# First pairs of heads in another order: fillers, gated V loads, flags and masks, and the casts of pair 8

## The chip, the cores and the metric

The kernel runs on one core of one Trainium2 chip. The metric is the device time of one execution in microseconds (us). The engines are TensorE (PE, its weight loads PEld), VectorE (DVE), ScalarE (ACT), GpSimd (POOL) and SyncE (SP, which here only issues transfers). Each works through its own instructions in program order.

## The reference, cut to what matters

Sparse attention over 8 batches x 8 heads, 576 positions, 64 wide, is followed by a two-layer feed-forward part:

```python
scores = scale * np.matmul(q, k.transpose(0, 1, 3, 2))
mask = np.abs(pos[:, None] - pos[None, :]) <= 32
mask = mask | is_global[:, None] | is_global[None, :]   # 8 global positions
attn = softmax(np.where(mask, scores, -1e9))
x = (attn @ v).transpose(0, 2, 1, 3).reshape(4608, 512)
r = np.maximum(x @ w_in, 0.0)            # 512 -> 2048
out = (s * (r * r) + b) @ w_out          # 2048 -> 512
```

All inputs and the output are float32 in DRAM; the 8 global positions are data.

## The kernel before, in words

Work goes by **pairs of heads**: 32 pairs p, four to a batch, and two pairs to a group m. For a pair, Q and K are transposed on TensorE (`trans_a` for K, `trans_b` for Q; from pair 8 on K comes transposed by a DMA instead, `turn_k`), the band of scores is computed in two pieces (`qk(p, 0)`, `qk(p, 1)`), ScalarE takes the exponential (`em`), VectorE multiplies the mask in, and `pvq` multiplies by V and sums; `norm_steps` divides and writes `xt`. The columns and rows of the 8 global positions are handled beside the band: they are gathered with an indirect DMA (`gather`), rounded, moved (`globals_of`) and put into V (`put_v`), K and Q (`put_kq`), and the global queries' rows are written into `xt` by GpSimd (`scatter`).

The feed-forward part is a generator, `moe_quanta`: each `next` (`lead()` in the first pairs, `Q()` later) emits one piece for 512 tokens, either a block of the first layer (psh, then a Relu on ScalarE and a square on VectorE) or a quarter of a block of rows of the second (pso). It fills TensorE between the attention steps.

The order of all engines is **written out by hand**. The first five pairs stand as straight code; from pair 5 on `run_pair` has eight slots a pair, and `at(s, ...)` puts extra steps at the end of slot s, ahead of that slot's piece of the feed-forward part. `later` collects evacuations that `flush` emits. `warm(n)` emits n matmuls on zeros of 128x512, called fillers here, whose result nobody reads; they go to the bank that `idle_bank` names.

**Loads.** SyncE loads V for all pairs and K and Q from pair 8 on (`load_v`, `load_nat`, `load_q`), as float32 in rows of 256 bytes for V and K. GpSimd loads K and Q of pairs 1 to 7 with a cast to bf16 (`load_kq`), the weights (`load_w_in`, `load_w_out`, later `wpiece` for the sum of w_out's rows), and the gathers. SyncE's transfers are on queue 1, GpSimd's on queue 0. The float32 tiles are cast afterwards: V with `cast_v` on VectorE, ScalarE or GpSimd, K with `round_k` and Q with `round_q` on ScalarE. A tile `gate` of one element is loaded by SyncE from `xgs[0]` ahead of V of pair 6; since SyncE issues in order, it holds all loads behind it until `xgs[0]` is written.

`band`, `gadd`, `vkey`, `kidx` (GpSimd) and `sel`, `isg`, `notg` (VectorE) are small tables from which `build_masks` makes the two masks.

Of the kernel before, what the change touches and what calls it, by code (L numbers as in the profile page):

```python
# [16 lines left out]
P = 128  # L17
# [61 lines left out]
def kernel(  # L79
# [186 lines left out]
    zero = const.tile([P, 1], FP32)  # L266
    nc.vector.memset(zero[:], 0.0)
# [10 lines left out]
    load_v(nc.sync, 0)  # L278
# [21 lines left out]
    for p in range(1, 6):  # L300
        load_v(nc.sync, p)
# [4 lines left out]
    load_kq(1)  # L306
    nc.vector.tensor_copy(out=row[:, 0:NG], in_=g32[:, :, 0])
# [52 lines left out]
    nc.gpsimd.memset(kidx[0:NG], 100000.0)  # L360
    vkey = const.tile([P, NCH], FP32)
# [11 lines left out]
    load_kq(2)  # L373
# [9 lines left out]
    gadd = const.tile([P, WM], FP32)  # L383
    nc.gpsimd.memset(gadd[:], 0.0)
    nc.gpsimd.memset(gadd[0:NG, WIN : WIN + P], 1.0)
    nc.gpsimd.memset(gadd[:, GAP : GAP + NG], 1.0)
    nc.gpsimd.memset(gadd[0:NG, GAP : GAP + NG], 0.0)
    load_kq(3)

# [7 lines left out]
    halves("q", nc.scalar.copy, 1)  # L397
    masks = []
# [34 lines left out]
    def globals_of(bb):  # L433
# [26 lines left out]
        def move(i):  # L460
            ps = bank("psv")
            ps = ps.rearrange("p (a h d) -> p a h d", a=4, h=2)
            for hp in range(4):
# [4 lines left out]
                lambda: nc.vector.tensor_copy(  # L468
# [67 lines left out]
    def trans_b(p, later=later):  # L536
        ps = trans("q", p)

        def evac():
            n = HB // NJ  # L540
            eng = A if p < 5 else V
# [212 lines left out]
    def lead():  # L754
        next(moe)
# [77 lines left out]
    def idle_bank():  # L833
        return fill[:, 0:DM]
# [31 lines left out]
    def turned(f, p):  # L866
# [4 lines left out]
    fill = ps_o.tile([P, 2 * DM], FP32, tag="o", name="psf")  # L871
    warm(7)
# [4 lines left out]
    )  # L877
    halves("k", nc.vector.tensor_copy, 0)
# [7 lines left out]
    rows_of(0)  # L886
    k_out = turned(trans_a, 0)
    warm(2)
    q_out = turned(trans_b, 0)
    put = select(0)  # L890
    warm(2)
    k_out()
    put()
    q_out()
    sel = const.tile([P, NCH, NG], FP32)
    nc.vector.tensor_tensor(
        out=sel[:], in0=view(kidx[:], [1, NCH], [0, NG]),
        in1=view(gidx_f, [0, NCH], [1, NG]), op=OP.is_equal,
    )
    isg = const.tile([P, NCH], FP32)  # L900
    nc.vector.tensor_reduce(out=isg[:], in_=sel[:], axis=AX.X, op=OP.add)
    notg = const.tile([P, NCH], FP32)
    nc.vector.tensor_tensor(out=notg[:], in0=vkey[:], in1=isg[:], op=OP.is_gt)
# [18 lines left out]
    for p in range(3):  # L922
        qk(p, 0)
        q_out = turned(trans_b, p + 1)
        warm((2, 2, 1)[p])
        if p == 0:
            for g in range(2):
                build_masks(g)
            nc.vector.memset(onesb[:], 1.0)
# [4 lines left out]
        warm((2, 1, 1)[p])  # L934
        k_out()
        put()
        flush()
        if p:
            cast_v(V, p - 1)
    qk(3, 0)  # L940
    turned(trans_b, 4)()
    qk(3, 1)
    mask_b = later.pop()
    flush()
    steps0[0]()
    steps0[2]()
    flush()
    put_v(V, 0)
# [196 lines left out]
```

## Time and profile before

| | |
|---|---|
| median of 3 runs | 351.9 us (350.98 to 353.53) |
| profiled execution | 352.85 us, its span 351.2 us |
| busy share of the span | PE 95%, PEld 48%, DVE 60%, ACT 59%, POOL 18% |
| transfers | 50.25 MB in 124,452 packets, mean 143 GB/s |
| on the chain that ended last | PE 71%, DMA 15%, DVE 5%, SyncE's queue 4%, ACT 2% |

The span is the time from the first to the last instruction that the profile shows. Busy time of matmuls is modelled at their ends. The chain is followed back from the last instruction, at each step to what released it.

### The profile page before, as it was taken

The page shows a single profiled execution, that of the slowest core. Times are in us where ns is not written, and L with a number is a line of the kernel's source. Part 1 is how long each engine was busy: PE and PEld are TensorE (multiplying, and loading weights), DVE is VectorE, ACT ScalarE, POOL GpSimd, SP SyncE. Part 2 cuts the span into 40 slices and gives each one's busy share as a digit, 9 for nine tenths or more (in the row PEclk, how much of TensorE's full clock was granted, in tenths as well). Part 3 has the DMA queues.
Part 4 walks back from the last instruction along what each step waited for, and adds up shares of the span by engine and source line. Part 5 has one row for each costly group of instructions (what it writes and reads, how often), then busy time and mean ns, then how long its engine had stood idle before and what let it go on. Part 6 is the DMA issues. An engine that isn't in the chain of part 4 may idle for free.

```text
span 351.2 us, 8783 instructions
## 1 busy us (share of the span) xinstructions
PE 333.5 (95%) x3433; PEld 170.2 (48%) x3433; DVE 211.0 (60%) x553; ACT 205.9 (59%) x347; POOL 64.0 (18%) x151
## 2 busy tenths in 40 slices
PE   8968999699999998899999999999999999999996
PEld 4545444344454544357644444444456544444444
DVE  5589777466748596647666767675757553513421
ACT  3455687538875787437874887488638604603600
POOL 7733832141003310130006000300020010000000
PEclk9985899999999999989999999999999999999999
DMA  7999999999989999999579998992730011011002
GB/s 156 198 207 198 197 209 190 201 169 225 170 183 143 221 211 165 210 134 173 91 151 252 184 173 183 240 196 58 153 112 2 2 63 61 0 62 60 1 32 89
DMA packets 124452, 50.25 MB, mean 143 GB/s; under 512 B 111378, under 2 KB 117714, under 8 KB 124402
## 3 DMA queue, kind: packets, MB, share of 16 engines
q1 hardware_dynamic: 115992, 38.45, 62.3%
q0 software_dynamic: 8064, 10.80, 16.3%
q8 instruction: 27, 0.44, 0.6%
q10 hardware_dynamic: 354, 0.43, 0.4%
q14 instruction: 15, 0.12, 0.1%
HBM read 42.35 MB, written 9.44 MB: 147 GB/s over the span
## 4 chain that ended last, share of the span: by engine, by line
PE 71%; DMA 15%; DVE 5%; SPq 4%; ACT 2%; issue 1%; POOL 0%; ACTq 0%; DVEq 0%
PE psh L687 31%; PE pso L721 29%; DMA natv<-in_v_dram 7%; DMA wst<-in_moe_w_out_dram 5%; PE po L592 5%; PE pss L568 4%; SPq L203 3%; DMA natq<-in_q_dram 2%; DVE wsum L1013 2%; DMA kt<-natb 1%; PE pst L501 1%; DVE xt L639 1%; ACT em L575 1%; PE psx L592 1%; DVE g L712 1%
## 5 line engine op out<-in xcount | busy, mean ns | idle before, releaser
L687 PE MATMUL psh<-xt,win_t 128*128 128x512 bf16 (+2 forms) x704 | 134.9, 342 | 0.6 <-DVE kt L527 0.6
L721 PE MATMUL pso<-wout_t,g 128*128 128x512 bf16 (+1 forms) x592 | 134.3, 377 | 0.0
L709 ACT ACTIVATE r<-psh 128x512 bf16<-128x512 f32 x144 | 85.3, 599 | 65.2 <-PE psh L687 64.4
L687 PEld LDWEIGHTS <-win_t 128*128 128x128 bf16 x704 | 62.4, 98 | 57.7 <-issue 3.0
L721 PEld LDWEIGHTS <-g 128*128 128x128 bf16 x592 | 55.2, 98 | 61.1 <-issue 1.7
L712 DVE TENSOR_TENSOR g<-r 128x512 bf16<-128x512 bf16 x144 | 60.9, 430 | 38.0 <-ACT r L709 37.1
L575 ACT ACTIVATE em<-pss 128x904 bf16<-128x904 f32 (+1 forms) x61 | 54.7, 897 | 39.9 <-PE pss L568 39.9
L576 DVE TENSOR_TENSOR em<-em,mask 128x904 bf16<-128x904 bf16 x64 | 39.0, 614 | 23.4 <-ACT em L575 23.3
L664 POOL COPY xt<-xg 128x4 bf16 (+1 forms) x72 | 18.0, 250 | 176.3 <-DVE xt L639 172.5
L741 DVE SCALAR_TENSOR_TENSOR osb<-pso,sb,bias_row 128x512 f32<-128x512 f32 (+1 forms) x25 | 18.1, 726 | 27.3 <-PE pso L721 27.2
L568 PE MATMUL pss<-qt,kt 64*128 64x160 bf16 (+1 forms) x366 | 22.9, 234 | 4.3 <-DVE qt L486 2.3
L568 PEld LDWEIGHTS <-kt 64*128 64x128 bf16 x384 | 11.6, 98 | 30.1 <-issue 15.9
L639 DVE TENSOR_TENSOR xt<-po,rep 128x480 bf16<-128x480 f32 (+2 forms) x60 | 24.4, 447 | 0.0
L646 ACT ACTIVATE ln<-po 128x324 f32<-128x324 f32 (+1 forms) x30 | 12.8, 426 | 10.7 <-PE po L592 10.7
L592 PE MATMUL po<-em,vring 128*32 128x160 bf16 (+3 forms) x840 | 18.0, 224 | 1.0 <-DVE vring L478 0.9
L214 ACT CAST natb<-natk 128x640 bf16<-128x640 f32 x24 | 17.4, 725 | 2.2 <-DMA natk<-in_k_dram 2.2
L543 DVE COPY qt<-pst 128x600 bf16<-128x600 bf16 x19 | 8.8, 464 | 11.8 <-PE pst L501 11.8
L592 PE MATMUL po<-em,onesb 128*32 128x192 bf16 (+2 forms) x360 | 11.8, 238 | 4.0 <-DVE xt L639 3.9
L592 PEld LDWEIGHTS <-vring 128*32 128x32 bf16 x896 | 14.6, 102 | 1.5 <-DVE vring L478 1.5
L649 ACT ACTIVATE rep<-ln 128x324 f32<-128x324 f32 (+1 forms) x32 | 14.7, 460 | 0.2
L1013 DVE TENSOR_TENSOR wsum<-wsum,wst 128x512 f32<-128x512 f32 x14 | 9.6, 685 | 7.5 <-DMA wst<-in_moe_w_out_dram 7.4
L238 ACT CAST sixq<-natq 120x640 bf16<-120x640 f32 x19 | 13.8, 729 | 0.0
(117 smaller groups left out, 217.5 us busy)
## 6 DMA issues: line engine op xcount, KB each, us to landing
natv<-in_v_dram SPq DMA_DIRECT2D x59, 150.0 KB
natk<-in_k_dram SPq DMA_DIRECT2D x47, 150.0 KB
out_dram<-osb SPq DMA_DIRECT2D x23, 256.0 KB
natq<-in_q_dram SPq DMA_DIRECT2D x37, 150.0 KB
wst<-in_moe_w_out_dram POOLq DMA_DIRECT2D x8, 512.0 KB, 6.8
out_dram<-osbh SPq DMA_DIRECT2D x9, 256.0 KB
win_t<-in_moe_w_in_dram POOLq DMA_DIRECT2D x4, 512.0 KB, 9.4
wout_t<-in_moe_w_out_dram POOLq DMA_DIRECT2D x4, 512.0 KB, 10.9
```

The costliest lines, as they stand in the source:

```text
L214: nc.scalar.copy(out=natb[:, p % NV].rearrange("p (c h d) -> p c h d", c=NCH, h=2), in_=natk[:, p % NV],)
L568: nc.tensor.matmul(ps[:, hh, at : at + hi - lo], ktile[p][r, P * c : P * c + P], qbufs[p % 3][r, lo:hi], start=at == 0, stop=at + hi - lo ...
L575: nc.scalar.activation(em[:], ps[:, :, 0:n], AF.Exp, scale=SCALE)
L576: later.append(lambda: nc.vector.tensor_mul(em[:], em[:], masks[g]))
L592: nc.tensor.matmul(po[DH * j : DH * j + DH, a : a + n], view(vring[:, p % NVR, c, hh, part - 1 :], [2, DH]) if part else onesb[:], emt[(p, ...
L639: nc.vector.tensor_tensor(out=view(xt[:, 2 * g, x0 + t0 :], [NXT, 2], [w, runs], [1, w]), in0=view(po[:, STEP[blk] + col :], [STEP[blk], 2 ...
L664: nc.gpsimd.tensor_copy(out=xt[:, h, S * (bi % NX) : S * (bi % NX) + S][:, :, ds(greg_p[i], 1)], in_=xgs[bi][:, h, i : i + 1],)
L687: nc.tensor.matmul(psh[:, d0 : d0 + n], win_t[:, a, f * P : f * P + P], xt[:, a, x0 : x0 + n], start=(a == 0 and j == 0), stop=(a == 3), s ...
L709: nc.scalar.activation(r[:], psh, AF.Relu)
L712: later.append(lambda g=g, r=r: nc.vector.tensor_mul(g[:], r[:], r[:]))
L721: nc.tensor.matmul(pso[:, 0:nn], gl[f][:, u * P : u * P + P], wout_t[:, f, n0 : n0 + nn], start=(f == 0), stop=(f == 15),)
L741: nc.vector.scalar_tensor_tensor(out=osb[:, 0:nn], in0=pso[:, 0:nn], scalar=s_bc, in1=bias_row[:, n0 : n0 + nn], op0=OP.mult, op1=OP.add,)
```

## The change

- The unused tile `zero` goes, so `dummy` is set first. The fillers ahead of the first scores become 5 + 2 in place of 7 + 2 + 2; those in the loop over the first pairs become one each in place of 2, 2, 1 and 2, 1, 1. Eight new ones stand further on: one between the two scores of pair 3, three ahead of `put_out(0, 0)`, three behind the transposes of pair 4's K, and one behind `steps0[1]`; those after pair 3 go to a bank of `ps_s`.
- SyncE loads V of pairs 0 to 5 behind a new gate, one element of K of pair 1, in place of V of pair 0 first and the others after the constants.
- On GpSimd the loads of pairs 2 and 3 move ahead of `vkey` and `band`; `gadd` moves to VectorE; the load of pair 6 moves ahead of the first scatter.
- `rows_of(0)` comes after the copy of pair 0's K. `gadd`, `sel`, `isg` and `notg` are made by `key_flags` on VectorE, in pair 0's turn of the loop at its end, with the masks behind it; pair 0's scores get their mask in the turn of pair 1.
- The second half of `gvx` is copied on ScalarE and made together with the first; pair 5's Q is copied on ScalarE; `cast_v(A, 4)` comes later; the first `lead()` stands between the scores of pair 4.
- `round_k(8)` moves from slot 4 of pair 6 to slot 6 of pair 5, `turn_k(8)` from slot 6 to slot 0 of pair 6, `round_q(8)` from slot 2 of pair 7 to slot 6 of pair 6. The loads of K and Q of pairs 10, 11 and 12 move to slot 1 of pair 6 and slots 4 and 5 of pair 7 (10 and 11 stood at the start of pairs 6 and 7, 12 at slot 4).

```diff
--- before.py
+++ after.py
@@ -263,8 +263,6 @@
 
-    zero = const.tile([P, 1], FP32)
-    nc.vector.memset(zero[:], 0.0)
     dummy = const.tile([P, DM], BF16)
@@ -275,7 +273,6 @@
     nc.sync.dma_start(out=sbrow[:, 1:2], in_=_bcast_dram(moe_b[:], 1))
-    load_v(nc.sync, 0)
     nc.sync.dma_start(
@@ -297,13 +294,15 @@
     )
-    for p in range(1, 6):
-        load_v(nc.sync, p)
 
     load_kq(1)
+    gate = const.tile([1, 2], BF16)
+    nc.sync.dma_start(out=gate[:, 0:1], in_=six["k"][0:1, 1, 0, 0, 0:1])
+    for p in range(6):
+        load_v(nc.sync, p)
     nc.vector.tensor_copy(out=row[:, 0:NG], in_=g32[:, :, 0])
@@ -358,6 +357,8 @@
     nc.gpsimd.memset(kidx[0:NG], 100000.0)
+    load_kq(2)
+    load_kq(3)
     vkey = const.tile([P, NCH], FP32)
@@ -370,7 +371,6 @@
     chop(vkey[:, NCH - 1 : NCH], 1, 0, last, -1, 0.0)
-    load_kq(2)
     band = const.tile([P, WM], FP32)
@@ -380,13 +380,6 @@
     nc.gpsimd.memset(band[:, GAP : GAP + NG], 0.0)
-    gadd = const.tile([P, WM], FP32)
-    nc.gpsimd.memset(gadd[:], 0.0)
-    nc.gpsimd.memset(gadd[0:NG, WIN : WIN + P], 1.0)
-    nc.gpsimd.memset(gadd[:, GAP : GAP + NG], 1.0)
-    nc.gpsimd.memset(gadd[0:NG, GAP : GAP + NG], 0.0)
-    load_kq(3)
-
     def halves(t, eng, h):
@@ -395,6 +388,23 @@
     halves("q", nc.scalar.copy, 1)
+    gadd = const.tile([P, WM], FP32)
+    sel = const.tile([P, NCH, NG], FP32)
+    isg = const.tile([P, NCH], FP32)
+    notg = const.tile([P, NCH], FP32)
+
+    def key_flags():
+        nc.vector.memset(gadd[:], 0.0)
+        nc.vector.memset(gadd[0:NG, WIN : WIN + P], 1.0)
+        nc.vector.memset(gadd[:, GAP : GAP + NG], 1.0)
+        nc.vector.memset(gadd[0:NG, GAP : GAP + NG], 0.0)
+        nc.vector.tensor_tensor(
+            out=sel[:], in0=view(kidx[:], [1, NCH], [0, NG]),
+            in1=view(gidx_f, [0, NCH], [1, NG]), op=OP.is_equal,
+        )
+        nc.vector.tensor_reduce(out=isg[:], in_=sel[:], axis=AX.X, op=OP.add)
+        nc.vector.tensor_tensor(out=notg[:], in0=vkey[:], in1=isg[:], op=OP.is_gt)
+
     masks = []
@@ -465,7 +475,7 @@
             later.append(
-                lambda: nc.vector.tensor_copy(
+                lambda: (A if i else V)(
                     out=gvx[bb][:, 512 * i : 512 * i + 512],
@@ -538,7 +548,7 @@
             n = HB // NJ
-            eng = A if p < 5 else V
+            eng = A if p < 6 else V
             if p >= NSIXQ:
@@ -831,7 +841,7 @@
     def idle_bank():
-        return fill[:, 0:DM]
+        return fill[0]
 
@@ -868,13 +878,14 @@
 
-    fill = ps_o.tile([P, 2 * DM], FP32, tag="o", name="psf")
-    warm(7)
+    fill = [ps_o.tile([P, 2 * DM], FP32, tag="o", name="psf")[:, 0:DM]]
+    warm(5)
     psi = spare[:, DM : DM + NG + 1]
     )
+    warm(2)
     halves("k", nc.vector.tensor_copy, 0)
@@ -883,24 +894,13 @@
     halves("q", nc.vector.tensor_copy, 0)
-    rows_of(0)
     k_out = turned(trans_a, 0)
-    warm(2)
     q_out = turned(trans_b, 0)
     put = select(0)
-    warm(2)
     k_out()
+    rows_of(0)
     put()
     q_out()
-    sel = const.tile([P, NCH, NG], FP32)
-    nc.vector.tensor_tensor(
-        out=sel[:], in0=view(kidx[:], [1, NCH], [0, NG]),
-        in1=view(gidx_f, [0, NCH], [1, NG]), op=OP.is_equal,
-    )
-    isg = const.tile([P, NCH], FP32)
-    nc.vector.tensor_reduce(out=isg[:], in_=sel[:], axis=AX.X, op=OP.add)
-    notg = const.tile([P, NCH], FP32)
-    nc.vector.tensor_tensor(out=notg[:], in0=vkey[:], in1=isg[:], op=OP.is_gt)
     gather(0, "kqv")
@@ -922,51 +922,61 @@
         q_out = turned(trans_b, p + 1)
-        warm((2, 2, 1)[p])
-        if p == 0:
-            for g in range(2):
-                build_masks(g)
-            nc.vector.memset(onesb[:], 1.0)
+        warm(1)
         q_out()
         put = select(p + 1)
-        warm((2, 1, 1)[p])
+        warm(1)
         k_out()
         put()
-        flush()
         if p:
+            flush()
             cast_v(V, p - 1)
+        else:
+            key_flags()
+            for g in range(2):
+                build_masks(g)
+            nc.vector.memset(onesb[:], 1.0)
+    load_kq(6)
     qk(3, 0)
     turned(trans_b, 4)()
+    warm(1)
     qk(3, 1)
     flush()
+    steps0[3]()
+    flush()
     put_v(V, 0)
     mask_b()
+    fill[0] = ps_s.tile([P, 2, DM], FP32, tag="s", name="psf")[:, 0]
+    warm(3)
     put_out(0, 0)
     put_v(V, 3)
-    steps0[1]()
     k_out = turned(trans_a, 4)
+    warm(3)
     step()
     put_out(1, 0)
+    steps0[1]()
+    gk_out = later.pop()
+    warm(1)
     step()
     scatter(0, 0)
-    load_kq(6)
     load_w_out(1)
     put_out(1, 1)
+    gk_out()
     k_out()
@@ -977,17 +987,14 @@
     qk(4, 0)
-    steps0[3]()
+    lead()
     qk(4, 1)
     flush()
-    gate = const.tile([1, 1], BF16)
-    nc.sync.dma_start(out=gate[:], in_=xgs[0][0:1, 2, 0:1])
+    nc.sync.dma_start(out=gate[:, 1:2], in_=xgs[0][0:1, 2, 0:1])
     load_v(nc.sync, 6)
     load_q(8)
-    cast_v(A, 4)
-    lead()
     first.close()
@@ -996,6 +1003,7 @@
     k_out()
+    cast_v(A, 4)
     lead()
@@ -1043,9 +1051,10 @@
             if j < NPAIR:
-                if j == 12:
-                    at(4, load_nat, nc.sync, "k", j)
-                    at(4, load_q, j)
+                if j in (10, 11, 12):
+                    x = {10: 1, 11: 4, 12: 5}[j]
+                    at(x, load_nat, nc.sync, "k", j)
+                    at(x, load_q, j)
                 elif j > 8:
@@ -1073,11 +1082,12 @@
                 at(3, turn_k, p + 2)
+        if p == 5:
+            at(6, round_k, 8)
         if p == 6:
-            at(4, round_k, 8)
-            at(6, turn_k, 8)
+            at(0, turn_k, 8)
+            at(6, round_q, 8)
         if p == 7:
-            at(2, round_q, 8)
             at(7, put_v, None, 8)
             at(7, put_v, None, p + 2)
```

## Rows read from the trace of the kernel before

**Rows 1.** Windows of 5 us: busy us (instructions) by engine, PEclk, DMA share, GB/s.

```profile
25.00:30.00 5.00, 3.43 (x92) 2.71 (x96) 4.70 (x15) 1.77 (x4) 0.00 (x0) 0.50 1.13 210
30.00:35.00 5.00, 3.99 (x101) 2.78 (x92) 4.82 (x18) 2.69 (x6) 3.00 (x11) 0.50 1.21 194
...
60.00:65.00 5.00, 3.18 (x62) 1.88 (x59) 0.78 (x1) 3.55 (x7) 0.72 (x1) 1.00 0.99 195
...
145.00:150.00 5.00, 2.94 (x20) 1.27 (x19) 4.63 (x14) 1.30 (x3) 1.02 (x4) 1.00 1.23 238
150.00:155.00 5.00, 5.00 (x27) 2.44 (x28) 2.50 (x4) 1.22 (x2) 2.39 (x6) 0.66 1.40 114
```

**Rows 2.** Timeline of TensorE, first 18 us: start, us, instructions.

```profile
1.42 3.17 PE L864 MATMUL psf<-dummy 128*128 128x512 bf16 x7 [1.42 <-DVE dummy L269]
...
15.19 0.69 PE L515 MATMUL pst<-ident,sixq 96*64 96x96 bf16 x12
...
17.19 0.45 PE L515 MATMUL pst<-ident,sixk 96*64 96x96 bf16 x12
```

**Rows 3.** The chain that ended last, 13 to 37 us: start, us, what.

```profile
13.59 11.88 DMA natv<-in_v_dram
...
27.17 1.05 PE psx L592 x30
...
31.22 1.27 PE psx L592 x40
...
34.86 1.93 PE psh L687 x4
```

**Rows 4.** Timeline of VectorE; in brackets the idle time before and its releaser.

```profile
8.60 0.19 DVE L896 TENSOR_TENSOR sel<-kidx,spread 128x40 f32<-128x40 f32 x1
...
26.60 0.88 DVE L257 CAST vring<-natv 128x640 bf16<-128x640 f32 x2
...
66.61 0.17 DVE L486 COPY kt<-gkt 128x40 bf16<-128x40 bf16 x1 [2.60 <-DMA kt<-natb]
```

**Rows 5.** Timeline of ScalarE, 48 to 62 us.

```profile
48.03 0.60 ACT L709 ACTIVATE r<-psh 128x512 bf16<-128x512 f32 x1
...
49.39 0.92 ACT L575 ACTIVATE em<-pss 128x904 bf16<-128x904 f32 x1
...
54.40 0.73 ACT L214 CAST natb<-natk 128x640 bf16<-128x640 f32 x1 [1.09 <-DMA natk<-in_k_dram]
...
61.12 0.83 ACT L243 CAST sixq<-natq 96x768 bf16<-96x768 f32 x1 [0.62 <-DMA natq<-in_q_dram]
```

**Rows 6.** Timeline of TensorE, 50 to 70 us.

```profile
50.91 0.36 PE L568 MATMUL pss<-qt,kt 64*128 64x92 bf16 x6
...
62.77 0.42 PE L509 MATMUL pst<-ident,sixq 96*128 96x96 bf16 x6 [1.82 <-ACT em L575]
...
66.92 0.37 PE L568 MATMUL pss<-qt,kt 64*128 64x160 bf16 x6 [0.28 <-DVE qt L486]
...
68.97 0.37 PE L592 MATMUL po<-em,onesb 128*32 128x92 bf16 x12 [1.68 <-DVE xt L639]
```

**Rows 7.** Timeline of SyncE's queue: start and length of issuing.

```profile
36.69 4.19 SPq L203 DMA_DIRECT2D natk<-in_k_dram  x2
...
62.34 1.66 SPq L249 DMA_TRANSPOSE kt<-natb  x1
```

**Rows 8.** GpSimd's loads of K, first 45 us (tile sixk): issue to landing.

```profile
DMA to landing us min/median/max: 5.9/7.0/10.6
```

**Rows 9.** DMA queue 1, windows 0:8, 0:16, 0:48, 54:58: packets, MB, share.

```profile
q1 hardware_dynamic: 1239, 0.63, 33.8%
...
q1 hardware_dynamic: 4271, 1.46, 48.0%
...
q1 hardware_dynamic: 9929, 2.88, 33.3%
...
q1 hardware_dynamic: 2187, 0.74, 81.1%
```


## The prediction

> **What bounds the kernel now.** I read the windows of 5 us first. TensorE is busy in nearly every one; what it lacks sits in four places: the first pairs of heads, 60 to 70 us, 135 to 150 us and the tail [rows 1]. Only the first two are touched by the change in more than order, so the question is what ends the waits there.
>
> The second view is the granted clock beside the matmuls themselves. From 25 to 35 us the clock is 0.50, that is 1.2 GHz, after a stretch in which TensorE had waited for VectorE and ScalarE several times [rows 1]. In the first 15 us the clock row says 1.00, but twelve transposes take 0.69 us there and 0.45 us from 17 us on, so I read the start as 1.2 GHz too [rows 2].
>
> The third is the chain that ended last. From 13.6 to 25.5 us it is a load of V, whose cast comes on VectorE at 26.6 us: V of pairs 2 and 3 lands some 1 us before it is wanted [rows 3, 4]. Then come TensorE at the low clock, and in 60 to 70 us transfers again: the Q of pair 9 [rows 5], and the transposed K of pair 8, for which VectorE waits until 66.6 us [rows 4]. TensorE's idle times there are 1.82, 0.28 and 1.68 us, 3.78 in sum [rows 6].
>
> The fourth is ScalarE's timeline, and it decides my forecast: the cast of pair 8's K (natb<-natk) ran at 54.40 us and had waited 1.09 us for the DMA of K [rows 5], though SyncE had issued that load from 36.69 to 40.88 us [rows 7]. So K of pair 8 landed at about 54.3 us.
>
> **The change part by part.** *Fillers.* Seven fillers take 3.17 us, 0.45 each [rows 2]. Ahead of the first scores eleven become seven: 1.8 us less. In the loop nine become six, and TensorE then waits for the copies that it covered. VectorE has its flags and the memsets of gadd added in pair 0's turn, and the masks behind the copies of pair 1's K instead of ahead: some seven small operations, each as the 0.19 us of one that moves with them [rows 4], 1.3 us. Bounds at the gather's cast (about 23 us): 1.8 earlier, or nothing; I take 0.5 earlier, the difference of the two.
>
> *Eight new fillers from pair 3's scores to the last `put_out` of the first batch.* At 1.2 GHz they cost 8 x 0.45 = 3.6 us, but fall mostly into waits of TensorE that exist: PE is busy 3.43 and 3.99 of 5 us in the two windows, 2.6 idle [rows 1]; so about 1.0 us net. If they bring the clock to 2.4 GHz, the longest runs of matmuls on the chain there (1.05 + 1.27 + 1.93 = 4.3 us [rows 3]) halve, 2.1 us. Bounds: 2.1 earlier to 1.0 later; I take 1.5 earlier, because the fillers of the loop were followed by such a rise at 17 us [rows 2]. The copy of half of gvx and of pair 5's Q to ScalarE relieves VectorE, which is the nearer bound; I count it within this.
>
> *V behind a gate.* SyncE now waits for K of pair 1 before it issues any V. Queued behind are all six V loads and, after them, everything else that SyncE loads. Those gpsimd loads took 5.9 us at least from issue to landing [rows 8], from an issue at 1.6 us: the gate opens at about 7.5 us, and V that was first issued at 2.0 comes 5 us later. By 8 us queue 1 had sent 1,239 packets [rows 9], of which about 300 are still sent; the deficit is 900. In exchange pairs 1 to 3 of K and Q are off the queues sooner, and GpSimd issues nothing large until the gathers are out, so V runs nearly alone for some 5 us: 547 packets per us (2,187 in 4 us) against 379 (4,271 less 1,239 in 8 us) [rows 9], 840 won back. The third V pair then lands between on time and, if nothing is won back, 900/177 = 5 us late (177 per us is what queue 1 sent from 16 to 48 us [rows 9]). I take on time, by the sum above; the margin is 1 us, so up to 4 us stay in the range as a stall of VectorE at its cast.
>
> The Trainium skill (DMA: Bandwidth & Descriptors, Anatomy of one DMA) gives a DMA from GpSimd about 2.0 us plus its bytes at 436 GB/s. By that the gate would open near 4.3 us (an estimate from that page) and the deficit be a third of mine; the row, 5.9 us at least, says otherwise, and I keep to it.
>
> *Loads of KQ 6 and weights.* The load of pair 6 moves ahead of the first scatter on GpSimd's queue, which is idle there until the scatter's xg is ready; nothing is issued later for it. Its bytes stand behind the same weights on queue 0 as before, so I cost it at nothing, and at up to 1 us for V if it displaces V's packets.
>
> *Pair 8.* The cast of its K goes from slot 4 of pair 6 to slot 6 of pair 5. In ScalarE's order that is just ahead of the Relu at 48.03 us [rows 5], six slots earlier. Queued behind it on ScalarE are Relus and the exponentials of pair 6. TensorE can go on to the second scores of pair 6 (50.91 us [rows 6]), which need the first exponential to have emptied their bank; there it stops until K has landed and the cast (0.73), two Relus (1.2) and that exponential (0.92) are through: landing + 2.9 us. Nothing in the change takes bytes from in front of this K: V of pairs 0 to 6 stands ahead of it on queue 1 as before, and the weights share the transfer engines as before. Bounds: 48 us, when queue 1 had sent 9,929 packets [rows 9], about as many as stand up to this load, and 58 us, if the deficit of V is carried whole (54.3 + 5, less the earlier second gate). I take 53, nearer to the observed 54.3.
>
> From 50.91 to 68.97 us TensorE worked 18.06 - 3.78 = 14.3 us [rows 6]. The later Q9 and K8 waits are then gone: by then Q9 has landed, and the transpose of K8, which SyncE issued at 62.34 behind three loads [rows 7], goes ahead of them. So TensorE passes the mark at landing + 2.9 + 14.3: 53 gives 70.2 us, 1.2 us later than before. The start's 2 us gain is swallowed by that wait, which has an absolute time.
>
> The wait is also long, 53 + 2.9 - 49 = 7 us. After the stall at 145 to 150 us the clock was 0.66 in the next 5 us, 1.7 us lost; with 3.2 busy of 5 in 60 to 65 us it stayed at 1.00 [rows 1]. Bounds 0 and 1.7; I take 0.8.
>
> *Later loads* (pairs 10 to 12, one to five slots later; Q8's cast earlier): no wait of TensorE in the places named above rests on them; nothing, and up to 1 us late if the loads come short. The wait at 135 to 150 us rests on weights for the sum of w_out, which the change doesn't touch.
>
> **Sum.** +1.2 + 0.8 = 2.0 us. The profiled execution took 352.85 us (span 351.2 and 1.65 around it), 0.95 above the median of the three runs; the changes add to the median: 351.9 + 2.0 = **353.9 us**.
>
> **The rivals.** *K of pair 8 is there in time (faster).* If queue 1 is ahead when the weights start, the early cast doesn't wait, the start's 2 us survive until pair 7, and the transposed K comes some 5 us earlier (its issue is no longer behind three loads). If Q9 still lands at 61.1 us, only 0.28 + 1.68 = 2.0 us are won; if it comes earlier too, 3.8 + 2.0 = 5.8. Middle: 3.9 us, 348.0. For it: the margin of V at 8 us is an estimate. Against: the load waited 13 us for its turn with both queues full.
>
> *V's deficit is carried (slower).* If queue 1 wins nothing back from 9 to 15 us, it stays 900 packets behind, and K of pair 8 lands near 58 us: landing + 17.2 = 75.2 against 68.97, 6.2 us later, and less by some 2 us that the queues of the weights have then ended earlier; 356.1 with no clock loss, 357.8 with all of it. It decides for "slower by over 1%" from a landing at 54.6 us on. For it: the weights' packets slowed queue 1 from 379 to 177 per us [rows 9]. The Trainium skill (DMA: Bandwidth & Descriptors, Queues, rings and completion order) says each transfer engine takes the queues in turn, packet by packet; by that rule small V packets lose against large weight packets, the rows agree, and it speaks against a change that moves V towards the weights.
>
> *Nothing arrives (same).* Landing at 51 to 52 us: block and removed waits cancel, 351 to 352.
>
> **How the numbers follow.** About 1%, 3.5 us, is what a measurement here can tell from no change. Forecast and cancelling case together 0.50 (landing 50 to 54.6 us); in time 0.25; deficit carried 0.25. In-time cases below 1% are few, the slow ones begin just above it: faster 0.23, same 0.50, slower 0.27. The range leaves a tenth on each side: 347 (4.9 of the 5.8 us won) to 358.
>
> **What would show it.** Right: ScalarE idle for 4 us or more before natb<-natk at about 46 us, released by the DMA of natk; TensorE idle at pair 6's second scores; no wait for kt at pair 8; a granted clock of 1.00 somewhere in 27 to 37 us. Wrong: that cast running without a wait, or a V cast of pairs 2 to 5 with a wait of several us, or the clock staying at 0.50 to 37 us with the fillers in.

## The result, and the profile after

The change makes the kernel 0.85% faster: 348.15 us (median of 20, 344.30 to 352.64) against 350.22 (20, 348.40 to 353.53), ratio 0.9915, 95% interval 0.9889 to 0.9941. That lies inside the forecast range (347 to 358), but the kernel became faster, where the forecast of 353.9 said 2.0 us slower. Ratios here leave out executions more than 1.5% above the fastest of the same kernel (two of four are left for e_kq6_back below, five of twelve for j_rest_only), so they are not the ratios of the medians (0.9941 here).

The two profiled executions differ by more than the kernels do: 345.3 us (span 343.7) after against 352.85 before. A second trace of each gave 348.82 and 350.0. So the main readings below are held against both traces of each kernel.

One time isn't in the views: the **landing** of pair 8's K. The traces keep the semaphore events of each transfer, up to 16 for each of the two halves of this K, and I take the last event that belongs to the load. Some events are missing in part of the traces.

The windows of 5 us of the kernel after, for [rows 1]:

```profile
25.00:30.00 5.00, 4.65 (x113) 2.77 (x113) 3.89 (x11) 3.00 (x6) 0.00 (x0) 1.00 1.16 201
30.00:35.00 5.00, 2.95 (x93) 1.93 (x95) 4.79 (x22) 2.78 (x6) 2.07 (x9) 1.00 1.20 189
...
60.00:65.00 5.00, 4.70 (x70) 2.55 (x72) 3.03 (x10) 3.07 (x6) 0.72 (x1) 1.00 1.20 194
...
145.00:150.00 5.00, 4.95 (x79) 3.46 (x78) 2.49 (x5) 2.40 (x4) 1.62 (x3) 1.00 0.96 145
150.00:155.00 5.00, 5.00 (x87) 3.92 (x85) 3.97 (x12) 4.16 (x8) 0.00 (x0) 1.00 1.56 200
```

TensorE is busy 4.70 of 5 us at 60 to 65 us, where it was 3.18 (4.95 against 3.51 in the second traces), and the hole at 145 to 150 us is gone too. That second hole is no part of the change: in the second trace of the kernel before, TensorE is busy 5.00 us in the same window.

ScalarE's timeline of the kernel after, for [rows 5]:

```profile
49.19 0.72 ACT L214 CAST natb<-natk 128x640 bf16<-128x640 f32 x1 [1.77 <-issue]
50.79 0.93 ACT L585 ACTIVATE em<-pss 128x904 bf16<-128x904 f32 x1
...
56.33 0.82 ACT L243 CAST sixq<-natq 96x768 bf16<-96x768 f32 x1
```

Its SyncE queue, for [rows 7]:

```profile
36.74 3.72 SPq L203 DMA_DIRECT2D natk<-in_k_dram  x2
...
56.99 2.14 SPq L249 DMA_TRANSPOSE kt<-natb  x1
```

The cast of pair 8's K ran at 49.19 us, behind a wait of 1.77 us. The profile gives this wait to no DMA, but K landed at 49.13 us, so it was for K. In the kernel before K landed at 54.37 us (54.02 in its second trace); the load was issued at the same time (36.7 us). The transposes of this K are issued at 56.99 instead of 62.34 (57.55 against 63.23 in the second traces). TensorE's timeline, for [rows 6]:

```profile
51.77 0.36 PE L578 MATMUL pss<-qt,kt 64*128 64x92 bf16 x6 [1.50 <-ACT em L585]
...
62.40 0.42 PE L519 MATMUL pst<-ident,sixq 96*128 96x96 bf16 x6 [0.25 <-ACT em L585]
...
66.21 0.37 PE L578 MATMUL pss<-qt,kt 64*128 64x160 bf16 x6
```

The early cast costs 1.50 us at the second scores of pair 6, and the waits of 1.82, 0.28 and 1.68 us shrink to 0.25 and below (1.44, 0.37 and 1.68 to 0.25 and below in the second traces). At the start pair 5's first scores run at 40.07 us, 0.73 earlier than before (40.80); in the second traces it is 39.55 against 41.42, but there the changed kernel loses 3.92 us at 44 us, as shown below.

### The profile page after: what moved, and what is told of

Read it like the earlier page. It is cut to its first block, busy times and chain, and to the rows that moved or that the text cites. A ratio compares the mean times of both kernels' runs of the same rounds, so it can differ in the third digit from the quotient of the medians.

```text
span 343.7 us, 8733 instructions
## 1 busy us (share of the span) xinstructions
PE 324.3 (94%) x3385; PEld 169.5 (49%) x3434; DVE 210.6 (61%) x554; ACT 206.8 (60%) x349; POOL 62.9 (18%) x147
## 4 chain that ended last, share of the span: by engine, by line
PE 77%; issue 5%; DMA 5%; DVE 4%; POOL 3%; ACT 2%; SPq 2%; POOLq 1%; ACTq 0%
PE pso L731 33%; PE psh L697 33%; PE po L602 5%; PE pss L578 4%; DMA natk<-in_k_dram 3%; DMA win_t<-in_moe_w_in_dram 2%; SPq L203 1%; PE pst L511 1%; DVE xt L649 1%; POOL sixq L178 1%; ACT em L585 1%; POOL gf L339 1%; ACT r L719 1%; POOL sixk L178 1%; POOLq L914 1%
## 5 line engine op out<-in xcount | busy, mean ns | idle before, releaser
L697 PE MATMUL psh<-xt,win_t 128*128 128x512 bf16 (+4 forms) x684 | 132.0, 340 | 2.5 <-issue 0.8
L731 PE MATMUL pso<-wout_t,g 128*128 128x512 bf16 (+1 forms) x568 | 129.2, 373 | 2.6 <-issue 2.1
L719 ACT ACTIVATE r<-psh 128x512 bf16<-128x512 f32 x144 | 85.2, 600 | 62.9 <-PE psh L697 60.1
L731 PEld LDWEIGHTS <-g 128*128 128x128 bf16 x592 | 54.9, 98 | 60.1
L602 PE MATMUL po<-em,vring 128*32 128x160 bf16 (+3 forms) x840 | 17.0, 218 | 0.0
L602 PEld LDWEIGHTS <-vring 128*32 128x32 bf16 x896 | 13.3, 96 | 0.0
L257 ACT CAST vring<-natv 128x640 bf16<-128x640 f32 x17 | 12.4, 730 | 0.0
```

The lines of the kernel that those rows point to most:

```text
L602: nc.tensor.matmul(po[DH * j : DH * j + DH, a : a + n], view(vring[:, p % NVR, c, hh, part - 1 :], [2, DH]) if part else onesb[:], emt[(p, ...
L697: nc.tensor.matmul(psh[:, d0 : d0 + n], win_t[:, a, f * P : f * P + P], xt[:, a, x0 : x0 + n], start=(a == 0 and j == 0), stop=(a == 3), s ...
L719: nc.scalar.activation(r[:], psh, AF.Relu)
L731: nc.tensor.matmul(pso[:, 0:nn], gl[f][:, u * P : u * P + P], wout_t[:, f, n0 : n0 + nn], start=(f == 0), stop=(f == 15),)
```

## The experiments

For all traces I use two marks: **A**, the start of ScalarE's 9th exponential of a score bank (pair 4), and **B**, that of the 17th (pair 8). From B on the traces differ by more than 1.5 us in two places only: at 133 to 150 us, and in pair 8 itself, by its slots. From B to the 33rd exponential the traces with the new slots take 68.6 to 70.1 us, those with the old ones 71.2 to 71.5 (j 74.1): there the new slots give some 2 us, whatever else is changed.

**Which part carries the gain?** a_pair8_back is the changed kernel with pair 8's slots and the loads of pairs 10 to 12 as before; d_pair8_only is the kernel before with those alone changed.

```diff
...
-        if p == 5:
-            at(6, round_k, 8)
         if p == 6:
-            at(0, turn_k, 8)
-            at(6, round_q, 8)
+            at(4, round_k, 8)
+            at(6, turn_k, 8)
         if p == 7:
+            at(2, round_q, 8)
```

> The changed kernel with the casts, the transpose and the loads of pairs 8 and 10 to 12 back in their old slots. Theory: in the changed kernel K of pair 8 lands at about 49 us, 5 us earlier than before, and the earlier slots turn that into the 2 to 3 us by which TensorE is ahead at 70 us; so this kernel should lose 1.5 to 3 us against the changed one (about 350 us) and show TensorE idle again for 2 us or more at pair 8's first scores, with the transposed K late. Rival: the slots don't matter, because the early landing alone removes the wait for Q of pair 9; then the time stays within 1 us of the changed kernel.

> The kernel before with only the slots of pairs 8 and 10 to 12 changed. Theory, as in the prediction: K of pair 8 lands at 54 us as in the kernel before, and ScalarE stops in front of its cast from 48 us until then; TensorE passes pair 8's second scores 1 to 3 us later than the kernel before (73 us or more) and the time is 0 to 3 us higher. Rival: the landing at 54 us is one execution's; then ScalarE waits less than 2 us and the time is 1 to 3 us lower than before.

Measured: a 349.96 us, ratio 1.0040 (1.0005 to 1.0075); d 351.86 us, 1.0026 (0.9985 to 1.0067). Without the slots the gain is gone, and the slots by themselves bring none. In a, though, TensorE didn't stand idle for 2 us at pair 8's first scores as expected: K landed at 46.84 us and its cast kept the late slot (54.40), and TensorE waited 1.68 us for VectorE at the product with V behind those scores. In d the forecast mechanism is there as it was written. ScalarE of d:

```profile
54.88 0.72 ACT L214 CAST natb<-natk 128x640 bf16<-128x640 f32 x1 [4.97 <-DMA natk<-in_k_dram]
```

TensorE of d:

```profile
51.95 0.81 PE L687 MATMUL psh<-xt,win_t 128*128 128x512 bf16 x3 [0.16 <-issue]
57.45 0.53 PE L568 MATMUL pss<-qt,kt 64*128 64x92 bf16 x6 [4.69 <-ACT em L575]
57.92 1.89 PE L687 MATMUL psh<-xt,win_t 128*128 128x512 bf16 x4
```

ScalarE waits 4.97 us for K, TensorE 4.69 us at the second scores of pair 6, which start 2.6 us after K's cast does (2.9 was forecast), and the four matmuls behind take 1.89 us instead of 1.04: half clock. So something else in the change must bring K earlier.

**Pair 6's load, or GpSimd's queue as a whole?** e_kq6_back is the changed kernel with that load put back, h_pair8_kq6 the kernel before with pair 8's slots and that load moved, k_kq6_only the load alone, j_rest_only the change without both.

```diff
+    load_kq(6)        # in h and k; e takes it back
     qk(3, 0)
...
     scatter(0, 0)
-    load_kq(6)
     load_w_out(1)
```

> The changed kernel with the load of pair 6's K and Q back between the first scatter and the weights behind it. Theory 1 (pair 6's bytes): 288 KB leave the burst of 33 to 42 us on GpSimd's queue, at the 200 GB/s of that stretch 1.4 us, and this is what lets K of pair 8 through; here its cast waits for the DMA until 51 to 54 us, TensorE waits at the second scores of pair 6, and the time is 349.5 to 351. Theory 2 (GpSimd's queue as a whole runs earlier because its weights are issued at 16.5 instead of 21.1 us): pair 6 makes no difference, the cast comes at 49 to 51 us without a DMA wait and the time stays at 348 to 348.5.

> The kernel before with the pair 8 slots of the change (as in d_pair8_only, 351.86 us, where the cast of K8 waited 4.97 us until 54.88) and with the load of pair 6's K and Q moved ahead of pair 3's scores, everything else as before. Theory 1 (pair 6's bytes): the cast comes at 51 to 53 us, its wait shrinks to 1 to 3 us, and the time falls to 349 to 350.5. Theory 2 (GpSimd's queue as a whole): the cast stays at 54 to 55 us with a wait of 4 us or more, the time at 351 to 352.5.

> The kernel before with the load of pair 6's K and Q moved ahead of pair 3's scores, and nothing else. Theory 1 (the gain is the early K of pair 8 together with the earlier slots that use it): K of pair 8 may land early here too, but its cast keeps the late slot at 54 us, so TensorE passes 66 to 72 us as before and the time is 349.5 to 351, ratio 0.997 to 1.003. Rival (the early load is a gain by itself, since V and Q behind it come earlier): 347.5 to 349, ratio 0.990 to 0.995.

> The changed kernel with both the load of pair 6 and the pair 8 slots as before: what is left are the fillers, the V gate, GpSimd's order at the start and VectorE's flags and masks. Theory 1 (all the gain is pair 6's load with pair 8's slots): 350 to 352, ratio 0.998 to 1.005. Rival (these parts bring the 2.0 us that the prediction gave them, and the traces of the changed kernel run at full clock from 26 us): 347.5 to 349, ratio 0.990 to 0.995.

Measured (medians in us, in brackets that of the kernel before in the same series):

| kernel | load of pair 6 | pair 8's slots | the rest | us (before) | ratio (95%) | K of pair 8 landed |
|---|---|---|---|---|---|---|
| d_pair8_only | old | new | old | 351.86 (349.71) | 1.0026 (0.9985 to 1.0067) | 54.86 |
| k_kq6_only | new | old | old | 348.76 (350.63) | 0.9954 (0.9920 to 0.9988) | 49.23 |
| h_pair8_kq6 | new | new | old | 347.52 (351.06) | 0.9905 (0.9868 to 0.9942) | 47.99 |
| j_rest_only | old | old | new | 354.21 (350.63) | 1.0004 (0.9955 to 1.0052) | 54.37 |
| a_pair8_back | new | old | new | 349.96 (349.71) | 1.0040 (1.0005 to 1.0075) | 46.84 |
| e_kq6_back | old | new | new | 354.00 (351.06) | 1.0113 (1.0013 to 1.0212) | 53.47 |
| the change | new | new | new | 348.15 (350.22) | 0.9915 (0.9889 to 0.9941) | 49.13 |

Two edits carry all of it: with the old start they give 0.9905, as much as the whole change. Pair 6's load decides when pair 8's K lands: at 53.5 to 54.9 us in all traces with the load in its old place, the two of the kernel before among them, and by 49.2 us in the four with the load early above. The slots turn that into time. The load of pair 6 gives 0.5% alone, where theory 1 had expected 349.5 to 351; 348.76 us is a time of the rival (347.5 to 349). In its trace the wait of 1.82 us at the transposes of 62.77 us [rows 6] is down to 0.67. h did better than theory 1 said (349 to 350.5). The rest of the change gives nothing at best: by medians e is 2.9 and j 3.6 us slower than the kernel before.

ScalarE of e, with the wait that theory 1 expected there:

```profile
53.54 0.72 ACT L214 CAST natb<-natk 128x640 bf16<-128x640 f32 x1 [2.71 <-issue]
```

GpSimd's queue in h:

```profile
23.94 0.71 POOL L178 DMA_DIRECT2D sixk<-in_k_dram  x1
24.58 0.71 POOL L178 DMA_DIRECT2D sixq<-in_q_dram  x1
...
35.18 0.76 POOL L418 DMA_DIRECT2D wout_t<-in_moe_w_out_dram  x1
...
40.66 1.52 POOL L418 DMA_DIRECT2D wout_t<-in_moe_w_out_dram  x2
```

ScalarE of h:

```profile
49.87 0.72 ACT L214 CAST natb<-natk 128x640 bf16<-128x640 f32 x1
```

What the two data queues of h sent from 40 to 44 us (packets, MB, share of the 16 engines' time):

```profile
q0 software_dynamic: 478, 0.39, 66.1%
q1 hardware_dynamic: 1927, 0.48, 62.3%
```

The same two queues in d, from 40 to 44 us:

```profile
q0 software_dynamic: 458, 0.46, 85.2%
q1 hardware_dynamic: 595, 0.15, 23.1%
```

In h, K of pair 8 is cast 5.0 us earlier than in d, and without a wait. Queue 1, which carries it, sent 1,927 packets in these 4 us against 595. Queue 0, with pair 7, the weights and in d also pair 6, sent about as many in both, but took 66.1% of the engines' time instead of 85.2%. In d queue 1 moved at about one packet for each of queue 0's (595 to 458). In h most of its 1,927 packets fall into a stretch in which queue 0 had little to send: from 41 to 43 us it is 1,500 against 156. In d there are two such stretches of one us, at 39 and at 44 us (440 against 89 and 718 against 85 packets). Pair 6's load, issued at 23.94 us in h, was issued at 35.42 in d, into this burst.

The packets can be counted. Pair 6's load is 2 x 144 KB in packets of 768 bytes, 384 of them. By 48 us queue 1 had sent 10,308 packets in h against 9,903 in d, and 10,303 in k against 9,929 in the kernel before: 405 and 374 more, about one for each packet that no longer stands in the burst. At the 150 packets per us that queue 1 gets beside the weights (598 in 4 us, last section) 384 packets are 2.6 us, less than the 5 to 7 us by which K came earlier, so the count explains a part of it and the rest stays open.

**The V gate and the late fillers.** b_ungated issues V as before; c_no_late_fillers takes out the eight fillers from pair 3 on.

```diff
...
     gate = const.tile([1, 2], BF16)                      # b
-    nc.sync.dma_start(out=gate[:, 0:1], in_=six["k"][0:1, 1, 0, 0, 0:1])
-    for p in range(6):
-        load_v(nc.sync, p)
...
     mask_b()                                             # c
-    fill[0] = ps_s.tile([P, 2, DM], FP32, tag="s", name="psf")[:, 0]
-    warm(3)
...
```

> The changed kernel with V of pair 0 first and V of pairs 1 to 5 behind the constants, with no gate. Theory: the gate gives the early landing of K and Q of the first pairs and, through them, everything that GpSimd issues afterwards; without it K of pair 8 lands at 52 us or later, ScalarE waits 3 us more in front of that cast, and the time rises by 1 to 3 us. Rival: the gate gives nothing (V comes 5 us later and is waited for at 28.6 us), the loads end with the same byte at the same time; then the time is the same within 1 us or up to 1 us lower, and K of pair 8 lands at 49 to 50 us.

> The changed kernel without the eight fillers from pair 3 on; those ahead of the scores and in the loop stay. Theory: they bring the clock to 2.4 GHz at about 26 us; without them matmuls from 27 to 37 us run at 1.2 GHz (40 matmuls of the products with V in 1.4 us and not 0.75), the first piece of the feed-forward part comes 1 to 2 us later, and the end 0 to 1.5 us later, since the wait for K of pair 8 at 49 us takes in part of it. Rival: VectorE sets the pace there, and the fillers only stand in TensorE's way; then the first piece comes at the same time or up to 1 us earlier.

> The changed kernel without the eight late fillers, a second trace. Theory clock: the 28 matmuls of pair 0's second V product at 27 to 28 us take 0.9 us or more (1.2 GHz) instead of 0.58, and the time is 349 to 352 with or without waits for DMA later. Rival (gap): those matmuls take 0.58 us as well, V of pair 5 or K of pair 8 waits 3 us or more, and a second trace without these waits would be at 346 to 348.

Measured: b 348.29 us, 0.9949 (0.9912 to 0.9986); c 350.37 us, 1.0004 (0.9964 to 1.0044); the second trace of c 346.52. The gate's worth is below what these intervals tell, and it isn't what brings K: in b, without it, K had landed at 48.26 us and was cast without a wait (52.31). The fillers do what they are meant to: the 28 matmuls of a V product at about 31 us take 0.58 us with them and 0.97 without. TensorE in the kernel after:

```profile
30.87 0.38 PE L602 MATMUL po<-em,onesb 128*32 128x160 bf16 x12 [0.92 <-DVE xt L649]
31.08 0.58 PE L602 MATMUL po<-em,vring 128*32 128x160 bf16 x28
```

TensorE in the second trace of c:

```profile
31.08 0.57 PE L602 MATMUL po<-em,onesb 128*32 128x160 bf16 x12 [1.06 <-DVE xt L649]
31.44 0.97 PE L602 MATMUL po<-em,vring 128*32 128x160 bf16 x28
```

The transposes of pair 4's K at 28 to 30 us say the same: twelve matmuls take 0.45 or 0.46 us in all nine traces with the eight fillers, and 0.69 us in all eleven without. Yet the second trace of c, without fillers, ended at 346.52 us. TensorE waits for VectorE in either, so a slow clock there is waited away. In c's first trace V of pair 5 waited 4.07 and K of pair 8 3.39 us (it landed at 53.63); in its second 0.60 and none. Theory clock was right on the matmuls (0.97 us), but not on the time: 349 us or more was due with or without waits. The rival was right on the time and wrong on the matmuls. Why the twelve times of c have so high a median isn't settled by one more execution.

**The two kernels again.**

> The kernel before once more, for a second trace. In the first one the 33rd and the 36th exponential of a score bank lie at 138.83 and 156.07 us, 17.2 us apart, where the four other kernels traced with full clock there need about 12.1 us. If that loss of 5 us at 140 to 150 us is usual for the kernel before, it is here again, and the change's gain would lie there. If it was an accident of that one execution, the distance is 12 to 14 us and the time 348 to 351 us. K of pair 8: cast at 54 to 55 us on ScalarE in either case; TensorE at 1.2 GHz from about 24 to 37 us.

> The changed kernel once more, for a second trace. If the early landing of pair 8's K belongs to the change, ScalarE casts it at 49 to 51 us again and TensorE has no wait of over 1.5 us before 60 us; the time is then 345 to 349. If it was an accident of the profiled execution, the cast comes at 53 to 55 us after a wait for the DMA, TensorE stops for 3 us or more at the second scores of pair 6, and the time is 349 to 352.

r_before2: 350.0 us, the 33rd and 36th exponential 13.55 us apart, not 17.24: the hole at 140 to 150 us was one execution's (11.85 to 13.57 us in the eighteen other traces). Its K of pair 8 landed at 54.02 us, as late as in the first trace, but nobody waited, as ScalarE came to the cast only then:

```profile
54.37 0.77 ACT L214 CAST natb<-natk 128x640 bf16<-128x640 f32 x1
```

r_after2: 348.82 us, and its ScalarE shows that the changed kernel doesn't always get its K early:

```profile
42.89 0.72 ACT L257 CAST vring<-natk 128x640 bf16<-128x640 f32 x1 [4.83 <-DMA natk<-in_v_dram]
53.54 0.73 ACT L214 CAST natb<-natk 128x640 bf16<-128x640 f32 x1 [1.28 <-DMA natk<-in_k_dram]
```

Of the eight traces with pair 6's load early and the weights where they were, K landed by 49.2 us in six, and at 53.5 us here and 53.6 in c. In these two V of pair 5, which stands ahead of K on queue 1, was late as well (cast at 42.9 and 42.5 us, by 40.3 in five of the others and without a wait at 43.4 in b).

**Holding the gap open.** If queue 1 gets through only while queue 0 pauses, weights issued later should help. i_h_weights_late and i_after_weights_late move the last two quarters of w_out behind the gather of batch 1; n takes out the late fillers as well, m adds them to i_h; o (from i_after) and p (from n) put the second half of w_in and the first quarter of w_out behind pair 6's load.

```diff
     load_kq(7)                  # i, m, n, o, p
-    load_w_out(2)
...
-    load_w_out(3)
     gather(1)
+    load_w_out(2)
+    load_w_out(3)
...
-    load_w_in(1)                # o, p
     load_kq(5)
-    load_w_out(0)
...
     load_kq(6)
+    load_w_in(1)
+    load_w_out(0)
```

> As h_pair8_kq6 (347.52 us), with the last two quarters of w_out issued behind the gather of batch 1 on GpSimd instead of ahead of it, 3 to 4 us later. Theory 1 (queue 1 sends V6 and K8 at 500 to 700 packets per us only until the last two quarters of w_out start, and at 145 per us afterwards): the gap is 3 to 4 us longer, K of pair 8 lands by 48 us in every execution, and the time is 345.5 to 347.5. Rival (the bytes are only exchanged): w_out lands 3 us later, TensorE waits for it at its first output matmuls at about 59 us, and the time is 348 to 350.5.

> The changed kernel with the same move of the last two quarters of w_out behind the gather of batch 1. Its second trace lost 4.8 us at V of pair 5 and 1.3 us at K of pair 8, its first trace did not; in both, queue 1 fell from 500 to 700 to about 145 packets per us when those quarters started. Theory 1: neither wait comes back, K of pair 8 lands by 48 us, and the time is 345 to 347, 1 to 3 us below the changed kernel's 348.15. Rival: TensorE waits for w_out at 58 to 60 us and the time is 348 to 350.

> As i_h_weights_late (347.45 us; the kernel before with pair 6's load early, pair 8's slots and the last weights behind the gather) with the eight late fillers of the change added and nothing else. Theory clock (the fillers keep TensorE busy so that it runs at 2.4 GHz from about 27 instead of 37 us): 1.0 to 2.5 us earlier, 345 to 346.5. Rival (TensorE waits for VectorE and V there, so a faster clock is waited away): 347 to 348, the same within the interval.

> As i_after_weights_late (346.84 us), without the eight late fillers. Theory clock: as much is lost as when they were taken out of the changed kernel, 2 to 3 us, 349 to 350. Rival (without fillers the last weights were issued half a us earlier and closed the gap before K of pair 8; behind the gather they can't): nothing is lost, 346.5 to 347.5, and K of pair 8 is cast without a wait by 50 us.

> n_nofill_weights_late once more, for more times beside the same executions of the kernel before: 345.5 to 346.5 and a ratio of 0.986 to 0.991 if it is below the changed kernel (0.9915), 347 to 348.5 if its six times were luck.

> As i_after_weights_late, with the second half of w_in and the first quarter of w_out issued behind pair 6's load, at about 22.5 us as in the kernel before, instead of 16.5 and 19 us. Theory (V of pair 3 waits in the changed start because those weights hold queue 1 at 90 packets per us from 18 to 28 us): VectorE's cast of V 3 runs at 26.5 to 28 us without a wait, the first lead comes 1 to 3 us earlier, 344 to 346.5. Rival (the weights are then late themselves): TensorE waits for win_t at its first lead at about 34 us, 347 or more.

> As n_nofill_weights_late (345.95 us), with the second half of w_in and the first quarter of w_out behind pair 6's load, as in o_w_in_late. If V of pair 3 is what is left of waits at the start, its cast runs at 27 to 28 us without a wait in every execution and the time is 344.5 to 346; if those weights then land too late or the wait only moves to V of pair 5, 346 to 347.5, no better than without.

Measured, with the start of the cast of pair 8's K and its landing:

| kernel | us | ratio (95%) | K cast | K landed |
|---|---|---|---|---|
| i_h_weights_late | 347.45 | 0.9911 (0.9872 to 0.9950) | 50.12 | 46.27 |
| i_after_weights_late | 346.84 | 0.9891 (0.9838 to 0.9943) | 49.74 | 48.00 |
| m_h_weights_fillers | 347.31 | 0.9909 (0.9875 to 0.9944) | 51.48 | 47.60 |
| n_nofill_weights_late | 345.95 (six times) | 0.9885 (0.9844 to 0.9926) | 47.19 | 46.69 |
| n2, the same again | 348.50 (twelve times) | 0.9952 (0.9912 to 0.9991) | 51.56 | 46.72 |
| o_w_in_late | 347.23 | 0.9908 (0.9873 to 0.9943) | 46.88 | 46.33 |
| p_both_late | 347.80 | 0.9894 (0.9836 to 0.9951) | 53.40 | 52.51 |

None is told apart from the changed kernel. n's 345.95 was luck, as n2 shows. K of pair 8 was cast without a wait in all seven traces, so the casts only bound its landing; by its events K was there by 48 us in six of them, as expected for i_h and i_after. p is the exception: there, and in n2, ScalarE waited for V of pair 5 instead (7.19 and 5.14 us). p's 347.80 lies above both of its ranges. So K's wait can be taken away and the time stays. m against i_h tests the fillers once more. TensorE of m, then of i_h:

```profile
31.97 0.58 PE L592 MATMUL po<-em,vring 128*32 128x160 bf16 x28
```

```profile
32.17 0.97 PE L592 MATMUL po<-em,vring 128*32 128x160 bf16 x28
```

The clock rises with them, and the time is the same (347.31 and 347.45), as the rival said. In o V of pair 3 didn't wait, as expected, but nor did it in n without that edit, and o's 347.23 lies in the rival's range. o's trace has the shortest span of all, 342.9 us; its times still run from 344.47 to 350.24. ScalarE of p:

```profile
35.71 0.72 ACT L257 CAST vring<-natk 128x640 bf16<-128x640 f32 x1
43.63 0.72 ACT L257 CAST vring<-natk 128x640 bf16<-128x640 f32 x1 [7.19 <-DMA natk<-in_v_dram]
```

The marks of the traces with pair 6's load early, in the order in which the second quarter of w_out was issued (us):

| trace | w_out(1) issued | cast of V 5 (its wait for the DMA) | A | B |
|---|---|---|---|---|
| p_both_late | 32.31 | 43.63 (7.19) | 32.33 | 70.79 |
| n2_nofill_weights_late | 33.18 | 42.51 (5.14) | 33.20 | 68.95 |
| c_no_late_fillers | 33.47 | 42.45 (4.07) | 33.49 | 73.69 |
| r_after2 | 33.86 | 42.89 (4.83) | 33.38 | 70.63 |
| n_nofill_weights_late | 34.00 | 39.43 (1.48) | 33.53 | 67.54 |
| o_w_in_late | 34.05 | 38.65 (0.63) | 33.58 | 66.26 |
| the kernel after | 34.48 | 39.42 (0.98) | 34.00 | 66.62 |
| c2_no_late_fillers | 34.70 | 39.40 (0.60) | 34.72 | 66.28 |
| k_kq6_only | 34.82 | 38.03 (0.35) | 34.85 | 67.22 |
| h_pair8_kq6 | 35.18 | 39.59 (1.37) | 35.20 | 67.26 |
| m_h_weights_fillers | 35.36 | 40.36 (2.63) | 34.90 | 68.88 |
| i_h_weights_late | 35.40 | 39.26 (0.81) | 35.43 | 67.51 |
| a_pair8_back | 36.22 | 40.30 (none) | 36.31 | 67.14 |
| i_after_weights_late | 36.28 | 40.78 (none) | 36.84 | 67.13 |
| b_ungated | 38.39 | 43.35 (none) | 38.95 | 69.70 |

This table is where the start's gain goes. In the lower eleven rows but b pair 4 begins anywhere from 33.5 to 36.8 us, and pair 8 at 66.3 to 67.5 in all but m (68.88): 3.3 us at A are 1.3 at B. b begins pair 4 last (38.95, behind a wait of VectorE for V of pair 3) and is late at B too. Of the four traces with the earliest start three are the latest of all at B, and the fourth, n2, is later than all lower rows but b. An earlier start issues the first scatter earlier, and the weights that stand behind it on GpSimd; where these came before 33.9 us, ScalarE waited for V of pair 5 until 42.4 to 43.6 us, elsewhere until 40.4 at most. That the weights' issue is the cause is read from fifteen traces, not tested by itself.

## Why the prediction was wrong

- **The step that failed** is *Loads of KQ 6 and weights*: "I cost it at nothing", and with it, under *Pair 8*, "Nothing in the change takes bytes from in front of this K". I counted the order within queue 0 and the bytes ahead within queue 1, and not the packets that queue 0 sends while K is on queue 1. The runs showed that this load decides when K lands: 53.5 to 54.9 us with it in its old place, by 49.2 us in six of eight traces with it early. The load was worth 0.5% alone and, with the slots, the step from 1.0026 to 0.9905, some 4 us.
- **Pair 8's mechanism** was right where its premise holds: in d K's cast ran at 54.88 us behind a 4.97 us wait, TensorE stopped 4.69 us, the clock fell to 0.50 in the window 55 to 60 us. That the forecast for the sum, 2.0 us slower, comes close to d's 2.15 above the kernel before (351.86 against 349.71 in the same executions) is in part luck. d's ratio can't tell it from no change, and in its trace the mark of the sum (the last of [rows 6]) came at 73.79 us, 3.9 and 4.8 us later than in the two traces of the kernel before; the new slots and the stretch from 133 to 150 us gave part of it back.
- **The changed kernel followed the rival** *K of pair 8 is there in time*, which had a chance of 0.25: 348.0 forecast, 348.15 measured. The match of the number is luck: the rival was to win 3.9 us from 351.9, the median of three executions, and 2.1 us were won from 350.22, the median of twenty. Its condition was put at the wrong place: "if queue 1 is ahead when the weights start". At 26 us queue 1 of the kernel after was about 1,100 packets behind (5,204 against 6,293) and still had K 5 us earlier. In the second trace of the changed kernel K landed at 53.48 us, as late as the sum took it, and V of pair 5 had held up TensorE before.
- **Fillers**, 0.5 and 1.5 us earlier: the late ones raise the clock, as the row of 0.58 us shows. Mis-sized: nothing in sum, since TensorE waits for VectorE there (347.31 with, 347.45 without in m and i_h). Pair 4 began at 34.00 and 33.38 us in the two traces of the changed kernel, at 33.36 and 34.65 in those of the kernel before, so next to nothing of the 2 us arrived at A. The rise of the clock at 17 us from which I took the 1.5 [rows 2] was one execution's: no other trace shows it, and in the second trace of the kernel before twelve transposes take 0.69 us from 15 to 30 us.
- **V gate**, nothing, with up to 4 us as a stall of VectorE at its cast. The gate opened at 7.82 us (7.5 forecast). Queue 1 was 979 packets behind at 8 us (900 forecast) and 434 at 16 us: 545 were won back, not 840. By 26 us it was 1,089 behind; w_out's first quarter was issued at 19.15 us now and at 23.78 before. The stall exists with the changed start (0.40 us in the kernel after, 3.90 in a, 4.43 in j, none in r_after2), but also without the gate (4.80 in b), so the gate alone isn't its cause. None of the traces with the old start shows it. It comes and goes between traces of one kernel, and its cause stays open.
- **V's deficit is carried** (356 to 358) fell: V of pair 3 was late by 0.40 us at most in the two traces of the changed kernel, and K landed at 49.13 and 53.48 us, not near 58.
- **The clock's 0.8 us** at the pair 8 wait: no loss in the kernel after, which waited 1.50 us there. In d, with 4.69, the five us from 55 on ran at 0.50 and the next five at 0.82; from TensorE's busy time there (2.54 and 4.95 us) I estimate 2.2 us.

## What to carry to other kernels

When two queues share the transfer engines and one carries large packets, don't count only the bytes ahead within a queue; count the packets that the other queue sends meanwhile, look for the stretches in which it has little to send, and see what a moved load does to both. A load that nobody waits for can be worth more than the waits that a change names. Before counting an earlier start as won, look for transfers that it triggers (here the weights behind the scatter) and for the transfer at which the next stage waits: in four traces here an earlier start came out later.

## What the runs showed of the hardware

With weights on queue 0 and K, Q and V on queue 1, the two sent about as many packets, though of different size. The two queues in the kernel after, 46 to 50 us:

```profile
q0 software_dynamic: 642, 0.63, 91.8%
q1 hardware_dynamic: 598, 0.15, 28.3%
```

That is 642 against 598 packets, 0.63 against 0.15 MB; from 40 to 42 us, with 140 packets on queue 0, queue 1 sent 1,407. The Trainium skill (DMA: Bandwidth & Descriptors, Queues, rings and completion order) says that each transfer engine takes the queues in turn, packet by packet; the trace agrees. It isn't so in every stretch: in d from 30 to 34 us, with the last V loads of the start on queue 1, it is 766 against 243 packets. How the packets divide among the 16 engines, these views don't show.

The clock's row said 1.00 for the kernel after from the first window on, while its twelve transposes took 0.69 us up to 24 us and 0.45 us from 28 us on in the same trace; in the second trace of c it said 1.00 from 30 to 35 us, where the 28 matmuls take 0.97 us. So ahead of its first change that row isn't to be trusted, and the length of like matmuls is.

VectorE of the kernel after stood still at the copy of pair 1's K, released by nothing that the trace names:

```profile
13.34 0.78 DVE L537 COPY kt<-pst 128x600 bf16<-128x600 bf16 x1 [5.09 <-remote]
```

In the second trace the same copy waited 4.84 us, put down to a matmul of TensorE (psg, L858); in a, c and p it waited 2.91 us for the transposes themselves, and pair 1 was earlier (the 4th exponential at 14.9 us against 16.6). What came on top in the kernel after stays open.
